# SwiGLU feed-forward on one core: the first weight slices move from two DMA queues to SyncE's alone

## The chip, the core and the metric

The kernel runs on one core of a Trainium2 chip. The metric is the device time of one execution in microseconds (us), lower is better. A core has five engines that run side by side, each with its own instruction stream: TensorE (PE; its weight loads are listed apart as PEld), VectorE (DVE), ScalarE (ACT), GpSimd (POOL) and SyncE (SP). A load or store is a DMA: an engine issues it in its own queue (here SyncE's, SPq, and ScalarE's, ACTq), 16 DMA engines move the data, and a semaphore tells when it has landed.

## What is computed

```python
# x: 1 x 2048 x 640, w_gate and w_up: 640 x 1536, w_down: 1536 x 640, all bfloat16
def reference(x, w_gate, w_up, w_down):
    g = _silu(x @ w_gate)
    u = x @ w_up
    return (g * u) @ w_down
```

## The kernel before

**Tiling.** The 2048 rows of x are worked in four blocks of 512 (`sb`), the 1536 hidden columns in twelve chunks of 128 (`fc`), the depth 640 in five chunks of 128 (`kd`). For each block and chunk, `proj` (L193 to L201) runs five matmuls of gate weights and five of up weights against the transposed x (`xT`, depth on the partitions), each filling a PSUM tile (`pg`, `pu`) of 128 x 512. `gate` (L208 to L215) applies silu on ScalarE (L212) and multiplies on VectorE (L213); the result `aT` feeds the down projection (L270 and L299). VectorE also works out the last four rows of x by itself (`row_dots`, L148), beside all this.

**How x is transposed.** Rows 0 to 255 are loaded as they are (`load_x`, L86, one DMA of 128 rows each), and transposed by TensorE in `transpose_chunk` (L186), from where ScalarE and VectorE copy them into `xT` (L191). All other rows come transposed by a DMA through the crossbar (`turn_x`, L110, a DMA_TRANSPOSE): rows 256 to 511 at the start, and each later block by one such load. In the text "the crossbar load" is that of rows 256 to 511.

**The start.** `head` (L217 to L251) writes out the order of TensorE's work on the first block and the first two chunks, and `keep_order` holds it: 18 warm-up matmuls on a tile of ones (L177), ten transposes of x rows 0 to 255 (L186), two more warm-up matmuls, 14 "early" gate matmuls (L237: 8 of 128 columns with the first two depth chunks, 6 of 256 columns with the other three), ten up matmuls over columns 0 to 255 (L195), and then, for each of the two chunks, five gate and five up matmuls over columns 256 to 511 (L195). These last need the crossbar load; the "late gate matmuls" are the first five of them. From then on the loop over blocks and chunks follows, with 512 columns per matmul.

**The order of the loads.** SyncE and ScalarE issue their DMAs in program order. The weights come in slices of hidden columns, `W_CHUNKS` = chunks 0 to 1, 2 to 3, 4 to 7 and 8 to 11, a gate and an up slice each. The first slices (256 columns, 320 KB each) are cut at depth chunk `K_CUT` = 2 into a part of 128 KB and one of 192 KB, and spread over both queues (L116 to L120):

- SyncE: x rows 0 to 127 (L86), gate depth 0 to 1 (L120), up depth 2 to 4 (L120), the crossbar load (L110), and then all later slices (L83), w_down (L126), the next block's crossbar load and the rest.
- ScalarE: x rows 128 to 255 (L86), gate depth 2 to 4 (L120), up depth 0 to 1 (L120), and then its first activation (L122), ahead of which it loads its table.

`turn_x(PE_X, SUB)` is the call that issues the crossbar load. The kernel has eight semaphores for these DMAs, taken in turn: a DMA that takes one again waits for the DMA that had it before, eight DMAs earlier.

Of the kernel before, what the change touches and what calls it, by code (L numbers as in the profile page):

```python
# [10 lines left out]
def _body(  # L11
# [8 lines left out]
    nc = tc.nc  # L20
# [12 lines left out]
    KD = D // P  # L33
# [10 lines left out]
    K_CUT = 2  # L44
    ROW_J = 0
    W_CHUNKS = [(0, 2), (2, 4), (4, 8), (8, 12)]
# [12 lines left out]
    wg_sb = consts.tile([P, KD, F], bf16)  # L59
    wu_sb = consts.tile([P, KD, F], bf16)  # L60
# [14 lines left out]
    wg_v = w_gate.rearrange("(kd p) f -> p kd f", p=P)  # L75
    wu_v = w_up.rearrange("(kd p) f -> p kd f", p=P)
    wd_v = w_down.rearrange("(kf p) d -> p kf d", p=P)

    def wslice(a, b):
        return slice(a * P, b * P)  # L80

    def load_w(eng, dst, src, a, b):
        eng.dma_start(out=dst[:, :, wslice(a, b)], in_=src[:, :, wslice(a, b)])  # L83
# [24 lines left out]
    def turn_x(c0, c1):  # L108
        s_sl = slice(c0 * P, c1 * P)
        nc.sync.dma_start_transpose(out=xT[:, :, s_sl], in_=xt_v[s_sl])  # L110
# [1 line left out]
    load_x(nc.sync, 0, 1)  # L112
    load_x(nc.scalar, 1, 2)
    f_sl = wslice(*W_CHUNKS[0])
    for dst, src, first, second in (
        (wg_sb, wg_v, nc.sync, nc.scalar),  # L116
        (wu_sb, wu_v, nc.scalar, nc.sync),
    ):
        for eng, k_sl in ((first, slice(0, K_CUT)), (second, slice(K_CUT, KD))):
            eng.dma_start(out=dst[:, k_sl, f_sl], in_=src[:, k_sl, f_sl])  # L120
    turn_x(PE_X, SUB)
    nc.scalar.activation(silu_first[:], ones[:, 0:1], ACT.Silu)  # L122
    for a, b in W_CHUNKS[1:]:
# [6 lines left out]
    def turn_w(dst, src):  # L130
# [7 lines left out]
        out=x_row[:],  # L138
        in_=x2[S - T : S, :].rearrange("t d -> (t d)").partition_broadcast(P),
# [114 lines left out]
    for sb in range(NSB):  # L254
# [27 lines left out]
        for q in range(P // Q):  # L282
            nc.scalar.dma_start(
                out=out2[
                    sb * S_BLK : sb * S_BLK + n_t, DA + q * Q : DA + (q + 1) * Q
                ].rearrange("(i r) c -> r i c", r=Q),
                in_=ot_q[q * Q : (q + 1) * Q, :].rearrange("r (i c) -> r i c", c=Q),
            )

        for j in range(SUB):  # L290
# [5 lines left out]
            for c0, c1, tag in cols:  # L296
# [10 lines left out]
                if c1 < D:  # L307
                    nc.scalar.copy(ot[:], po[:])  # L308
                    eng = nc.sync
                else:  # L310
                    nc.vector.tensor_copy(out=ot[:], in_=po[:])  # L311
                    eng = nc.scalar
# [81 lines left out]
def kernel(tc, *args):  # L394
    _body(tc, *args)
    tc.close()
    tc.compile()
    _trim(tc.nc)
# [30 lines left out]
```

## Time and profile before

| what | value |
|---|---|
| three runs, median (lowest to highest) | 163.66 us (163.46 to 163.86) |
| profiled execution: span from first to last instruction | 162.2 us |
| what lies around it (median less span) | 1.5 us |
| TensorE busy | 159.8 us, 798 matmuls |
| VectorE busy | 110.9 us |
| ScalarE busy | 42.7 us |
| gate and up matmuls of L195 | 58.5 and 59.8 us |
| DMA traffic | 15.86 MB, mean 98 GB/s |
| first matmul that reads w_up | starts at 5.80 us |
| first matmul that reads the crossbar load | starts at 6.92 us |

The profile is that of one execution; its own time isn't listed apart from its span, so the 1.5 us is the difference to the runs' median. "Busy" is the time in which an engine had an instruction under way. The chain that ended last is followed back from the last instruction: at each step to what released it, or to the instruction before it on its engine; the view gives shares of the span. The table of waits adds up, for each pair, how long an engine sat idle and what ended that. The timeline lists instructions in order of time: start, duration, engine, line, operation, output <- input, shape and count, all in us from the span's start. The DMA view lists issues with their sizes and the median time from issue to landing.

### The profile page before, as it was taken

The page shows a single profiled execution, that of the slowest core. Times are in us where ns is not written, and L with a number is a line of the kernel's source. Part 1 is how long each engine was busy: PE and PEld are TensorE (multiplying, and loading weights), DVE is VectorE, ACT ScalarE, POOL GpSimd, SP SyncE. Part 2 cuts the span into 40 slices and gives each one's busy share as a digit, 9 for nine tenths or more (in the row PEclk, how much of TensorE's full clock was granted, in tenths as well). Part 3 has the DMA queues.
Part 4 walks back from the last instruction along what each step waited for, and adds up shares of the span by engine and source line. Part 5 has one row for each costly group of instructions (what it writes and reads, how often), then busy time and mean ns, then how long its engine had stood idle before and what let it go on. Part 6 is the DMA issues. An engine that isn't in the chain of part 4 may idle for free.

```text
span 162.2 us, 2118 instructions
## 1 busy us (share of the span) xinstructions
PE 159.8 (99%) x798; PEld 77.9 (48%) x798; DVE 110.9 (68%) x249; ACT 42.7 (26%) x74; POOL 0.6 (0%) x6
## 2 busy tenths in 40 slices
PE   9999999999999999999999999999999999999995
PEld 8854444444444444444444444444444444445454
DVE  2042233599469999979919999979964999993000
ACT  5132222112222222221222322221214222222121
POOL 1000000000000000000000000000000000000000
PEclk9999999999999999999999999999999999999999
DMA  7999999994179992003110000000320000000312
GB/s 208 258 339 348 362 218 249 219 234 94 34 185 178 224 195 61 4 0 34 65 65 0 0 4 2 0 0 2 63 69 32 0 0 0 0 0 4 50 39 73
DMA packets 42441, 15.86 MB, mean 98 GB/s; under 512 B 33216, under 2 KB 42304, under 8 KB 42432
## 3 DMA queue, kind: packets, MB, share of 16 engines
q1 hardware_dynamic: 33536, 14.72, 37.7%
q10 hardware_dynamic: 8896, 1.02, 4.1%
q8 instruction: 6, 0.10, 0.2%
q14 instruction: 3, 0.02, 0.1%
HBM read 6.88 MB, written 2.62 MB: 59 GB/s over the span
## 4 chain that ended last, share of the span: by engine, by line
PE 99%; DVE 0%; issue 0%
PE pu L195 32%; PE pg L195 31%; PE po_a L299 26%; PE po_t L270 6%; PE pw L177 1%; PE pg L237 1%; PE pt L186 1%; DVE ot_b L311 0%; DVE ones L106 0%
## 5 line engine op out<-in xcount | busy, mean ns | idle before, releaser
L195 PE MATMUL pu<-xT,wu_sb 128*128 128x512 bf16 (+2 forms) x250 | 59.8, 370 | 0.0
L195 PE MATMUL pg<-xT,wg_sb 128*128 128x512 bf16 (+2 forms) x240 | 58.5, 374 | 0.0
L213 DVE TENSOR_TENSOR aT<-sg,pu 128x512 bf16<-128x512 f32 (+1 forms) x48 | 32.8, 683 | 32.8 <-PE pu L195 28.1
L212 ACT ACTIVATE sg<-pg 128x512 f32<-128x512 f32 (+1 forms) x48 | 28.6, 596 | 71.2 <-PE pg L195 68.1
L299 PE MATMUL po_a<-wd_sb,aT 128*128 128x512 bf16 (+2 forms) x216 | 42.8, 358 | 0.0
L148 DVE SCALAR_TENSOR_TENSOR prod<-wgT,x_row 128x640 f32<-128x640 bf16 x48 | 39.4, 821 | 1.1
L148 DVE SCALAR_TENSOR_TENSOR prod<-wuT,x_row 128x640 f32<-128x640 bf16 x48 | 39.4, 822 | 1.0
L195 PEld LDWEIGHTS <-wu_sb 128*128 128x128 bf16 x250 | 24.4, 98 | 27.6 <-DMA wu_sb<-in_w_up_dram 0.3
L195 PEld LDWEIGHTS <-wg_sb 128*128 128x128 bf16 x240 | 23.5, 98 | 26.9
L299 PEld LDWEIGHTS <-aT 128*128 128x128 bf16 x216 | 20.7, 98 | 21.6
L308 ACT CAST ot<-po_a 128x512 bf16<-128x512 f32 (+1 forms) x17 | 9.5, 560 | 32.0 <-PE po_a L299 20.8
L270 PE MATMUL po_t<-aT,wd_sb 128*128 128x512 bf16 (+1 forms) x48 | 10.4, 366 | 0.0
L270 PEld LDWEIGHTS <-wd_sb 128*128 128x128 bf16 x48 | 4.7, 98 | 5.1
L311 DVE CAST ot_b<-po_a 128x128 bf16<-128x128 f32 x1 | 0.3, 291 | 9.9 <-PE po_a L299 9.9
L279 ACT CAST ot_t<-po_t 128x512 bf16<-128x512 f32 (+1 forms) x4 | 2.2, 558 | 11.6 <-PE po_t L270 11.6
L148 DVE DVE_READ_ACCUMULATOR prod<-wuT,x_row 128x1 f32 x48 | 3.9, 82 | 0.0
L148 DVE DVE_READ_ACCUMULATOR prod<-wgT,x_row 128x1 f32 x48 | 3.9, 82 | 0.0
L281 DVE STREAM_TRANSPOSE ot_q<-ot_t 128x512 bf16<-128x512 bf16 (+1 forms) x4 | 2.7, 678 | 1.7 <-ACT ot_t L279 1.7
L177 PE MATMUL pw<-ones 128*128 128x128 bf16 x20 | 2.5, 313 | 0.4 <-DVE ones L106 0.4
L191 DVE COPY xT<-pt 128x384 bf16<-128x384 bf16 x2 | 0.7, 358 | 2.9 <-PE pt L186 2.9
L237 PE MATMUL pg<-xT,wg_sb 128*128 128x128 bf16 (+1 forms) x14 | 2.3, 360 | 0.0
L177 PEld LDWEIGHTS <-ones 128*128 128x128 bf16 x20 | 2.1, 148 | 0.4 <-DVE ones L106 0.4
(15 smaller groups left out, 7.6 us busy)
## 6 DMA issues: line engine op xcount, KB each, us to landing
wd_sb<-in_w_down_dram SPq DMA_DIRECT2D x1, 1920.0 KB, 14.5
out_dram<-ot SPq DMA_DIRECT2D x15, 128.0 KB, 1.7
wg_sb<-in_w_gate_dram SPq DMA_DIRECT2D x2, 640.0 KB, 7.7
wu_sb<-in_w_up_dram SPq DMA_DIRECT2D x2, 640.0 KB, 8.7
x_row<-in_x_dram SPq DMA_DIRECT2D x1, 640.0 KB, 4.7
out_dram<-ot_q ACTq DMA_DIRECT2D x12, 32.0 KB, 1.9
wg_sb<-in_w_gate_dram SPq DMA_DIRECT2D x1, 320.0 KB, 4.9
wu_sb<-in_w_up_dram SPq DMA_DIRECT2D x1, 320.0 KB, 5.4
```

The costliest lines, as they stand in the source:

```text
L148: nc.vector.scalar_tensor_tensor(out=prod[:], in0=wT[:, fc, :], scalar=1.0, in1=x_row[:, t, :], op0=ALU.mult, op1=ALU.mult, accum_out=acc[ ...
L177: nc.tensor.matmul(pw[:, 0:P], lhsT=ones[:], rhs=ones[:], start=True, stop=True)
L186: nc.tensor.transpose(out=pt[:, kd - k0, :], in_=x_sb[:, c, kd * P : (kd + 1) * P], identity=ident[:],)
L195: nc.tensor.matmul(ps[:, c0:c1], lhsT=w_sb[:, kd, fc * P : (fc + 1) * P], rhs=xT[:, kd, sb * S_BLK + c0 : sb * S_BLK + c1], start=(kd == 0 ...
L212: nc.scalar.activation(sg[:, 0:n_s], pg[:, 0:n_s], ACT.Silu)
L213: nc.vector.tensor_tensor(out=aT[:, fc, s0 : s0 + n_s], in0=sg[:, 0:n_s], in1=pu[:, 0:n_s], op=ALU.mult)
L237: nc.tensor.matmul(pg[:, c0:c1], lhsT=wg_sb[:, kd, wslice(fc, fc + 1)], rhs=xT[:, kd, c0:c1], start=(kd == 0 and c0 == 0), stop=(kd == KD ...
L270: nc.tensor.matmul(po_t[:], lhsT=wd_sb[:, kf, DA:D], rhs=aT[:, kf, sb * S_BLK : sb * S_BLK + n_t], start=(kf == 0), stop=(kf == KF - 1),)
L279: nc.scalar.copy(ot_t[:], po_t[:])
L281: nc.vector.transpose(out=ot_q[:], in_=ot_t[:])
L299: nc.tensor.matmul(po[:], lhsT=aT[:, kf, s0 : s0 + P], rhs=wd_sb[:, kf, c0:c1], start=(kf == 0), stop=(kf == KF - 1),)
L308: nc.scalar.copy(ot[:], po[:])
```

## The change

The four DMAs of the first gate and up slices become three, all issued by SyncE: gate depth 0 to 1, gate depth 2 to 4, and the whole up slice in one DMA by `load_w` (a helper that exists before, L83). They stand where SyncE's two parts stood, so the crossbar load comes behind all of them in SyncE's queue. ScalarE issues x rows 128 to 255 alone and goes on to its first activation. No instruction of TensorE, VectorE or GpSimd is changed, and what is computed stays the same.

```diff
     load_x(nc.sync, 0, 1)
     load_x(nc.scalar, 1, 2)
     f_sl = wslice(*W_CHUNKS[0])
-    for dst, src, first, second in (
-        (wg_sb, wg_v, nc.sync, nc.scalar),
-        (wu_sb, wu_v, nc.scalar, nc.sync),
-    ):
-        for eng, k_sl in ((first, slice(0, K_CUT)), (second, slice(K_CUT, KD))):
-            eng.dma_start(out=dst[:, k_sl, f_sl], in_=src[:, k_sl, f_sl])
+    for k_sl in (slice(0, K_CUT), slice(K_CUT, KD)):
+        nc.sync.dma_start(out=wg_sb[:, k_sl, f_sl], in_=wg_v[:, k_sl, f_sl])
+    load_w(nc.sync, wu_sb, wu_v, *W_CHUNKS[0])
     turn_x(PE_X, SUB)
     nc.scalar.activation(silu_first[:], ones[:, 0:1], ACT.Silu)
```

## The prediction

> **What bounds the kernel now.** First the page: its busy time and its chain of waits.
>
> ```profile
> span 162.2 us, 2118 instructions
> ...
> PE 159.8 (99%) x798; PEld 77.9 (48%) x798; DVE 110.9 (68%) x249; ACT 42.7 (26%) x74; POOL 0.6 (0%) x6
> ...
> PE 99%; DVE 0%; issue 0%
> ```
>
> TensorE (PE) is busy in 99% of the span and carries 99% of the chain that ended last. A load matters only where a matmul waits for it. So I looked next at the table of who waited for whom, for anything on PE or its weight loads (PEld) that ends on a DMA. There is one row:
>
> ```profile
> PEld L195 <- DMA wu_sb<-in_w_up_dram: 0.3, 1, 0.3
> ```
>
> Once, for 0.3 us, a weight load waited for the first slice of w_up, one of the loads that this change moves. The timeline of the first 8 us says how much of that PE lost (start, duration, engine, line, operation). From it I took SyncE's issues (SPq), ScalarE's (ACTq) and three matmul groups:
>
> ```profile
> 0.00 0.40 SPq L86 DMA_DIRECT2D x_sb<-in_x_dram  x1
> 0.12 0.41 ACTq L86 DMA_DIRECT2D x_sb<-in_x_dram  x1
> ...
> 0.46 0.42 SPq L120 DMA_DIRECT2D wg_sb<-in_w_gate_dram  x1
> 0.57 0.45 ACTq L120 DMA_DIRECT2D wg_sb<-in_w_gate_dram  x1
> ...
> 0.92 0.47 SPq L120 DMA_DIRECT2D wu_sb<-in_w_up_dram  x1
> 1.04 0.51 ACTq L120 DMA_DIRECT2D wu_sb<-in_w_up_dram  x1
> 1.43 1.63 SPq L110 DMA_TRANSPOSE xT<-in_x_dram  x1
> ...
> 3.11 0.57 SPq L83 DMA_DIRECT2D wg_sb<-in_w_gate_dram  x1
> ...
> 3.61 2.34 PE L237 MATMUL pg<-xT,wg_sb 128*128 128x128 bf16 x14
> ...
> 5.80 1.29 PE L195 MATMUL pu<-xT,wu_sb 128*128 128x256 bf16 x10
> ...
> 6.92 0.71 PE L195 MATMUL pg<-xT,wg_sb 128*128 128x256 bf16 x5
> ```
>
> The reader is to see three meeting points. The DMA view gives issue to landing, which I add to the issue times:
>
> - w_gate, first part (128 KB): 0.46 + 2.8 = 3.3; second part (192 KB): 0.57 + 3.6 = 4.2. The 14 early gate matmuls begin at 3.61, and the first of them that needs the second part at 4.47. No wait.
> - w_up: 1.04 + 4.7 = 5.7 (ScalarE's part) and 0.92 + 4.7 = 5.6. The up matmuls begin at 5.80.
> - the crossbar load (turn_x of x rows 256 to 511): 1.43 + 5.4 = 6.8. The first matmul that reads it starts at 6.92. This is the closest one: 0.1 us to spare.
>
> **The change part by part, with costs.**
>
> *w_up, the wait that goes.* Without the wait PE would go on when its 14 gate matmuls are through. The 18 warm-up matmuls of 128 columns start at 0.40 and the next group at 2.29: 105 ns each. Eight of the 14 have 128 columns and six 256: 8 x 0.105 + 6 x 0.21 = 2.1 us, so they are done with the array at 3.61 + 2.1 = 5.72 to 5.75. The up matmuls start at 5.80. PE itself lost 0.05 us; the rest of the 0.3 is PEld, which runs ahead. So **at most 0.05 us** can be won here at PE's present pace.
>
> Does w_up land in time? Ahead of its end stand x (320 KB), w_gate (320 KB) and itself (320 KB), 0.98 MB. The rates of the half-microsecond stretches from 1.0 to 4.5 us (159, 352, 322, 254, 282, 284, 315 GB/s) sum to 0.98 MB, so the data is in at about 4.5 us, whichever queue holds it. One queue alone is no slower: from 6.5 to 8.3 us only SyncE's queue moves data, 275 GB/s. Data to landing is about 0.5 us (the crossbar load's last 256-byte packet ends at 6.29 in the DMA records, and it lands at 6.82). So w_up lands at 4.9 to 5.2, ahead of 5.72. It stays ahead up to 0.5 us of error; past that the 0.05 is not won.
>
> *w_gate.* Its second part goes to SyncE, issued at 0.92 instead of 0.57. It no longer shares with w_up, which now stands behind it. x, w_gate: 640 KB by the same rates is in at about 3.4, landed at 3.8 to 4.0, needed at 4.36 (its weight load). Nothing.
>
> *ScalarE.* It loses two issues (0.45 + 0.51 us) and starts its table load (1.28 us, now at 1.58) at about 0.6. What it does next, the copy of transposed x at 2.99, would be ready some 0.25 us sooner, but the gate matmul that reads it starts only when PE has passed the transposes and two gap matmuls. PE is busy there, so nothing.
>
> *The crossbar load, moved past one more issue.* SyncE now issues x, two gate parts (0.42 and 0.45 to 0.47) and the whole w_up slice (320 KB; the row at 3.11 for that shape takes 0.57). Issues start at 0.00, 0.46, 0.92, 1.43 and, for turn_x, **2.03 instead of 1.43**. In its ring it stands behind 320 KB of w_up instead of 192. No trace row shows this order, so I bound the landing:
>
> - earliest: data starts when w_up's is in, 4.5. From 5.5 to 6.0 us, with nothing but this load moving, 566 packets went: 1,132 per us. Its 1,280 packets (256 rows of 1,280 bytes by 256) take 1.13 us: 5.6, landed 6.1.
> - latest: the same 5.4 us from issue as now, 2.03 + 5.4 = 7.4. A little under it lies its own stretch of now, 4.10 (first packet in the DMA records) to 6.82, 2.7 us, from 4.5: 7.2. That stretch holds a stop: 760 packets in the microsecond from 4.1, then 62 in the 0.3 us from 5.1.
> - nearest row: the crossbar load of 512 rows issued at 44.88 has its first packet at 46.18 and lands at 5.1 from issue, 49.98, 3.8 us for 2,560 packets. Half of it is 1.9: 6.4.
>
> I take 6.6, between the nearest row and the row that holds the stop. PE, with the 0.05 won, needs it at 6.87. So it stays hidden, by a quarter of a microsecond; past 6.87 every 0.1 us of lateness costs 0.1.
>
> The Trainium skill (DMA: Bandwidth & Descriptors, Latency and other measured facts) gives 261 GB/s for a transposing DMA with a non-contiguous middle dimension, by which these 0.33 MB would take an estimated 1.26 us and land at about 6.3; the load's own stretch here, 2.7 us, is 120 GB/s and does not agree.
>
> *What is queued behind.* The next slices go out after turn_x, so some 0.6 us later: 3.71 instead of 3.11 for w_gate columns 256 to 511. But their data waits for the crossbar load's anyway. That slice lands at 3.11 + 4.9 = 8.0 now and its matmuls start at 9.11; w_up's at 3.73 + 5.4 = 9.1 against 10.19. Both have 1 us of cover, more than the 0.6. The slices behind (10.9 and 13.0 against 13.4 and 14.5) have more than that. All later issues keep their order, and nothing that PE does changes.
>
> **Sum.** -0.05 (w_up) + 0 + 0 + 0 = -0.05 us: the span goes from 162.17 to 162.12. The three runs have a median of 163.66, 1.5 above the profiled span, for start and end, which the change leaves alone: **163.6 us**.
>
> **The rivals.**
>
> *Slower: the crossbar load is late.* One mechanism: its landing follows its issue, not the bytes ahead, so 0.6 us later issue means 7.2 to 7.4. It decides from 6.87 on. PE would start the late gate matmuls 0.1 after landing, at 7.5 instead of 6.92: +0.4 to +0.6, 164.0 to 164.3. For it: the load is now the closest of all, and its issue is the only thing that moves back. Against it: now its first packet leaves only at 4.10, 2.7 us after the issue, against 1.3 at 44.88, so it waits in the ring, not for the issue.
>
> *Faster: PE's slow phase ends sooner in other executions.* The matmuls start 105 ns apart per 128 columns early on, but from 9.11 to 10.19 five of 512 columns take 1.08 us, 54 ns per 128. The pace doubles about when the up matmuls start (between 5.5 and 5.9), though the profile's granted clock reads 1.00 throughout. If in another execution it doubles 1 to 2 us sooner, PE reaches the up matmuls 0.5 to 1 us sooner; the kernel before can't use that, as w_up lands at 5.7. The changed kernel can, until the crossbar load's landing: the late gate matmuls start at 6.5 to 6.7 instead of 6.92, -0.25 to -0.45 us, 163.2 to 163.4. For it: the runs lie 0.4 us apart, and something moves them. Against it: it needs both an early doubling and a crossbar load by 6.5, and the one trace has the doubling at 5.5 to 5.9. The Trainium skill (TensorE: Matmul & The Clock Gate, Part 1: The HAM clock gate) has a rule for this rival: the clock doubles at the end of a busy 3.4 us window that runs free of the kernel's start, so its place would differ from run to run; one trace can't show that.
>
> *Nothing at all:* the parts of w_up are held by the crossbar load's traffic in the new order too and land at 5.6 or later: 0, 163.7. This has the forecast's sign within what can be told.
>
> **How the numbers follow.** About 0.2% (0.33 us) is what a measurement of this kernel can tell from no change. Forecast and "nothing at all" together 0.46; the crossbar load late by over 0.33 us net 0.27; the early doubling with a gain over 0.33 us 0.27. Unlike signs hold much of the chance, so the forecast's own range is 163.4 to 163.8. The whole range goes down to 163.1 (the faster rival at its full 0.45 and 0.1 for the runs' spread) and up to 164.25 (the slower rival at 0.6).
>
> **What would show it.** In the profile after: w_up landing by 5.2, with no PEld row waiting for it; turn_x issued near 2.03 and landed by 6.87; the late gate matmuls within 0.1 us of 6.87; the chain still 99% PE. A PE or PEld row that waits for xT's DMA, or late gate matmuls past 7.1, would show the slower rival; up matmuls at 5.5 or sooner and late gate matmuls by 6.6 the faster one. The forecast is wrong if matmuls from 9 us on wait for weights, which would mean the covers of 1 us did not hold.

## The result and the profile after

| kernel | median of 10 runs each | lowest to highest |
|---|---|---|
| before | 163.51 us | 163.14 to 163.86 |
| changed | 164.27 us | 163.95 to 164.51 |

The change makes the kernel slower by 0.76 us, ratio 1.005 (95% interval 1.0039 to 1.006). The forecast was -0.05 us at 163.6, 163.4 to 163.8 as its own range; the time lies just over the top of the whole range, 164.25. The profiled execution has a span of 163.0 against 162.2.

The page of the changed kernel, its span, the busy time and the chain that ended last, by engine and by line:

```profile
span 163.0 us, 2117 instructions
...
PE 159.7 (98%) x798; PEld 77.6 (48%) x798; DVE 110.9 (68%) x249; ACT 42.9 (26%) x74; POOL 0.6 (0%) x6
...
PE 95%; DMA 3%; SPq 1%; DVE 0%; issue 0%
PE pu L192 32%; PE pg L192 31%; PE po_a L296 26%; PE po_t L267 6%; DMA wu_sb<-in_w_up_dram 3%; SPq L116 1%; SPq L86 0%; DVE ot_b L308 0%
```

PE works as long as before (159.7 against 159.8 us). What is new is in the chain: 3% is a DMA, the first w_up slice, and 1% the issue of the gate parts ahead of it. So the time was added in the start, by waiting, and the table of waits says for what:

```profile
PEld L234 <- DMA wg_sb<-in_w_gate_dram: 0.8, 1, 0.8
PE pg L234 <- DMA wg_sb<-in_w_gate_dram: 0.6, 1, 0.6
...
PEld L183 <- DMA x_sb<-in_x_dram: 0.5, 1, 0.5
PEld L192 <- DMA wu_sb<-in_w_up_dram: 0.4, 1, 0.4
...
PE pt L183 <- DMA x_sb<-in_x_dram: 0.2, 1, 0.2
...
PE pu L192 <- DMA wu_sb<-in_w_up_dram: 0.2, 1, 0.2
```

PE now waits for both slices that were moved. It also waits 0.2 us for x rows, whose load was not moved; e1 comes back to that. The timeline of the changed kernel places it (line numbers are three lower than before):

```profile
0.45 0.93 SPq L116 DMA_DIRECT2D wg_sb<-in_w_gate_dram  x2
0.54 1.28 ACT L119 ACT_TABLE_LOAD   x1 [0.54 <-issue]
...
1.42 0.49 SPq L83 DMA_DIRECT2D wu_sb<-in_w_up_dram  x1
...
1.95 3.29 SPq L110 DMA_TRANSPOSE xT<-in_x_dram  x1
...
3.96 0.92 PE L234 MATMUL pg<-xT,wg_sb 128*128 128x128 bf16 x8
...
5.47 0.83 PE L234 MATMUL pg<-xT,wg_sb 128*128 128x256 bf16 x6 [0.59 <-DMA wg_sb<-in_w_gate_dram]
...
6.46 1.26 PE L192 MATMUL pu<-xT,wu_sb 128*128 128x256 bf16 x10 [0.16 <-DMA wu_sb<-in_w_up_dram]
...
7.74 0.71 PE L192 MATMUL pg<-xT,wg_sb 128*128 128x256 bf16 x5
```

The up matmuls start at 6.46 instead of 5.80 and the late gate matmuls at 7.74 instead of 6.92. That 0.82 is the whole difference of the spans; the next group starts at 9.91 against 9.11 and nothing is lost or regained behind it. The DMA view of the changed kernel (issue to landing) gives the landings:

```profile
wu_sb<-in_w_up_dram SPq DMA_DIRECT2D x1, 320.0 KB, 5.0
wg_sb<-in_w_gate_dram SPq DMA_DIRECT2D x1, 192.0 KB, 4.5
...
xT<-in_x_dram SPq DMA_TRANSPOSE x1, 5.7
```

w_gate's second part: 0.91 + 4.5 = 5.4 (before 4.2). w_up: 1.42 + 5.0 = 6.4 (5.7). The crossbar load: 1.95 + 5.7 = 7.7 (6.8). All three are late, and the w_up slice alone holds PE until 6.46 + ten matmuls at 0.11 = 7.57; the crossbar load, landed at 7.69, adds the last 0.17.

Why are they late, with the same bytes? The busy time by stretches of 0.75 us shows it (stretch, its length, PE busy and instructions, granted clock, DMA share, GB/s), first of the kernel before:

```profile
2.50:3.25 0.75, 0.75 (x9) 1.00 0.94 268
3.25:4.00 0.75, 0.75 (x10) 1.00 0.99 278
4.00:4.75 0.75, 0.75 (x9) 1.00 1.31 304
```

and of the changed kernel:

```profile
2.50:3.25 0.75, 0.54 (x6) 1.00 1.00 280
3.25:4.00 0.75, 0.75 (x10) 1.00 0.69 186
4.00:4.75 0.75, 0.75 (x10) 1.00 0.86 181
```

From 3.25 us the DMA engines move a third less, and are busy for 0.69 of the time where they were for 0.99, though every load of the first slices had been issued by 1.91. This hole is what the experiments are about.

### The profile page after: what moved, and what is told of

It is laid out like the page before. It is cut to its first block, busy times and chain, and to the rows that moved or that the text cites. A ratio compares the mean times of both kernels' runs of the same rounds, so it can differ in the third digit from the quotient of the medians.

```text
span 163.0 us, 2117 instructions
## 1 busy us (share of the span) xinstructions
PE 159.7 (98%) x798; PEld 77.6 (48%) x798; DVE 110.9 (68%) x249; ACT 42.9 (26%) x74; POOL 0.6 (0%) x6
## 3 DMA queue, kind: packets, MB, share of 16 engines
HBM read 6.88 MB, written 2.62 MB: 58 GB/s over the span
## 4 chain that ended last, share of the span: by engine, by line
PE 95%; DMA 3%; SPq 1%; DVE 0%; issue 0%
PE pu L192 32%; PE pg L192 31%; PE po_a L296 26%; PE po_t L267 6%; DMA wu_sb<-in_w_up_dram 3%; SPq L116 1%; SPq L86 0%; DVE ot_b L308 0%
## 5 line engine op out<-in xcount | busy, mean ns | idle before, releaser
L234 PE MATMUL pg<-xT,wg_sb 128*128 128x128 bf16 (+1 forms) x14 | 1.7, 280 | 0.6 <-DMA wg_sb<-in_w_gate_dram 0.6
```

The costliest lines, as they stand in the source:

```text
L234: nc.tensor.matmul(pg[:, c0:c1], lhsT=wg_sb[:, kd, wslice(fc, fc + 1)], rhs=xT[:, kd, c0:c1], start=(kd == 0 and c0 == 0), stop=(kd == KD ...
```

## The experiments

All numbers in one table. "Rate" is the GB/s from 3.25 to 4.00 us. "Copies" is the start of the last of the 1,280 packets of 512 bytes that carry the first gate and up slices, "crossbar" the landing of the crossbar load, both from the DMA records and semaphores of the one profiled execution (us). The ratio is to the kernel before on the same chip.

| kernel | rate | copies | crossbar | median us | ratio (95%) |
|---|---|---|---|---|---|
| before | 278 | 5.12 | 6.82 | 163.51 | |
| changed | 186 | 6.00 | 7.69 | 164.27 | 1.005 (1.0039 to 1.006) |
| e1, changed | 152 | 6.17 | 7.87 | 164.47, one run | |
| e9, changed | 198 | 5.97 | 7.67 | 164.17 | 1.003 (1.0013 to 1.0048) |
| e2 up on ScalarE | 343 | 4.60 | 6.31 | 163.92 | 1.0044 (1.0014 to 1.0074) |
| e3 late issue | 330 | 4.58 | 6.57 | 163.69 | 1.002 (1.0002 to 1.0038) |
| e4 plain x | 106 | | | 165.22 | 1.0107 (1.0068 to 1.0146) |
| e5 gate part on ScalarE | 290 | 5.57 | 7.31 | 163.51 | 0.9968 (0.9927 to 1.0008) |
| e6 up part on ScalarE | 290 | 5.19 | 6.86 | 163.75 | 1.0019 (0.9975 to 1.0063) |
| e7 gate part and up on ScalarE | 216 | 8.14 | 9.11 | 168.26 | 1.0219 (1.011 to 1.0328) |
| e8 gate in one | 305 | 4.93 | 6.65 | 163.97 | 1.0026 (0.9999 to 1.0053) |
| e10 gate in one | 317 | 5.35 | 7.07 | 163.69 | 1.0016 (0.9995 to 1.0036) |
| e11 cut at 1 | 240 | 5.74 | 7.44 | 165.92 | 1.0126 (1.0077 to 1.0175) |
| e12 cut at 4 | 272 | 4.95 | 6.64 | 163.70 | 1.0011 (0.9994 to 1.0028) |
| e13 x on ScalarE | 353 | 4.89 | 6.57 | 165.05 | 1.0083 (1.005 to 1.0116) |
| e14 cut at 4, part on ScalarE | 296 | 4.73 | 6.41 | 163.62 | 0.9993 (0.9977 to 1.001) |
| e15 tiny between | 143 | 5.92 | 7.59 | 164.63 | 1.0084 (1.005 to 1.0119) |

**e1: is it of the change?** The changed kernel, nothing edited.

> The changed kernel as it is, for a second profile. What has to come back if it is of the change and not of one execution: the second part of w_gate lands after 4.8 us (5.42 in the first profile of it), w_up after 6.0 (6.42), the crossbar load after 7.3 (7.69). What may differ: x rows 0 to 127 landed at 2.66 there against 2.25 in the kernel before, though nothing ahead of them changed; if that is of one execution, they land by 2.4 here. About 164.3 us either way.

The second gate part landed at 5.46, w_up at 6.60, the crossbar load at 7.87: it is of the change. x rows 0 to 127 landed at 2.66 again, against 2.25 in the profile before; but e3, whose first loads are those of the kernel before, has 2.55, and e12 2.13. So I don't count it to the change, and PE waits for gate behind it in any case.

**e2: the up slice in the other queue.**

```diff
-    load_w(nc.sync, wu_sb, wu_v, *W_CHUNKS[0])
+    load_w(nc.scalar, wu_sb, wu_v, *W_CHUNKS[0])
```

> The changed kernel with the whole first w_up slice in ScalarE's queue behind x rows 128 to 255; both gate parts stay on SyncE's, and the crossbar load is issued at about 1.43 again. Theory A (the copies ahead end late when they all stand in one queue, and the crossbar load can't flow before the last of them has ended): copies spread over two queues end by 5.2, the crossbar load lands by 7.0, 163.4 to 163.7. Theory B (the crossbar load lands a fixed time after its issue): 1.43 + 5.4 = 6.8, the same 163.4 to 163.7. If a whole w_up slice in one DMA is itself the trouble: over 164.0.

The copies and the crossbar load came as early as theory A says; 6.31 is half a microsecond sooner than theory B has it. The time did not follow: 163.92. The view of waits has PE waiting 0.35 us for the second gate part, which landed at 5.21: ScalarE issued w_up at 0.53, SyncE the gate part at 0.91, and w_up's packets went first. Whether that comes from the order of issue, or from the gate part's place as the third load of SyncE's queue (e15 below), this run doesn't tell. Theory B gets its own run next.

**e3: the issue alone is late.** The kernel before with this ahead of `turn_x(PE_X, SUB)`:

```diff
+    tiny = consts.tile([P, 2, 8], bf16)
+    for n in range(2):
+        nc.sync.dma_start(out=tiny[:, n, :], in_=x_v[:, 0, n * 8 : n * 8 + 8])
     turn_x(PE_X, SUB)
```

> The kernel before, with two tiny loads (16 bytes per partition, into a tile that nothing reads) on SyncE's queue just ahead of the crossbar load, so that it is issued 0.8 to 1.0 us later, 2.2 to 2.4 instead of 1.43, and all else stays on both queues. Theory A (it waits for the last copy ahead, not for its issue): landing within 0.2 us of 6.8, 163.4 to 163.8. Theory B (fixed time after its issue): lands at 7.6 to 7.8, late gate matmuls at 7.7 to 7.9, 164.3 to 164.5.

The crossbar load became the ninth DMA of eight semaphores, and so was issued later than meant. From the timeline and the DMA view of e3, its issue and its time to landing:

```profile
3.01 1.46 SPq L110 DMA_TRANSPOSE xT<-in_x_dram  x1
```

```profile
xT<-in_x_dram SPq DMA_TRANSPOSE x1, 3.6
```

Issued 1.6 us later than before, it landed at 6.57, 0.25 us *sooner*. Theory B, a fixed time from issue, is refuted. The 0.2% that e3 loses has its own row in the timeline of e3: the next gate slice, issued behind the crossbar load, is late now.

```profile
9.33 1.25 PE L198 MATMUL pg<-xT,wg_sb 128*128 128x512 bf16 x4 [0.37 <-DMA wg_sb<-in_w_gate_dram]
```

**e4: no transposing load behind the copies.** The crossbar load of the changed kernel is a plain load here, which leaves these rows untransposed:

```diff
-    turn_x(PE_X, SUB)
+    nc.sync.dma_start(
+        out=xT[:, :, PE_X * P : SUB * P],
+        in_=x2[PE_X * P : SUB * P, :]
+        .rearrange("(p two) d -> p (two d)", two=2)
+        .rearrange("p (k c) -> p k c", k=KD),
+    )
```

> The changed kernel with the crossbar load replaced by a plain load of the same 320 KB into the same tile, so that these rows are not transposed and the outputs of rows 256 to 511 are not the reference's; it tells what the copies do without a transposing load behind them. If one queue alone makes the copies end late: w_gate's second part still lands after 4.8 and w_up after 6.0, about 163.8 to 164.2. If it is the crossbar load behind them that holds them up: w_gate's second part by 4.2, w_up by 5.3, 163.0 to 163.5.

The hole is there without the crossbar load, deeper even. The stretches of e4:

```profile
2.50:3.25 0.75, 0.75 (x8) 1.00 0.78 201
3.25:4.00 0.75, 0.75 (x10) 1.00 0.51 106
```

w_gate's second part landed at 5.26 and w_up at 7.17, so the kernel is slower than expected, 165.22. The 16 increments of w_up's semaphore came between 4.62 and 7.17: the DMA engines have drifted apart by 2.5 us, and those that were ahead went on with the next slices. The crossbar load does not make the hole.

**e5 and e6: half undone.** In e5 the second gate part, in e6 the first up part is back in ScalarE's queue:

```diff
-    nc.sync.dma_start(out=wg_sb[:, K_CUT:KD, f_sl], in_=wg_v[:, K_CUT:KD, f_sl])
+    nc.scalar.dma_start(out=wg_sb[:, K_CUT:KD, f_sl], in_=wg_v[:, K_CUT:KD, f_sl])
```

```diff
-    load_w(nc.sync, wu_sb, wu_v, *W_CHUNKS[0])
+    nc.scalar.dma_start(out=wu_sb[:, 0:K_CUT, f_sl], in_=wu_v[:, 0:K_CUT, f_sl])
+    nc.sync.dma_start(out=wu_sb[:, K_CUT:KD, f_sl], in_=wu_v[:, K_CUT:KD, f_sl])
```

> The change half undone: gate depth 2 to 4 back in ScalarE's queue behind x rows 128 to 255; gate depth 0 to 1 and the whole up slice on SyncE's. Theory A' (a single queue leaves the DMA engines without work from about 2.7 to 4 us, while its next load is not yet being served, and only loads of the other queue fill that): the 192 KB of ScalarE's queue fill it, 250 GB/s or more from 3.25 to 4.00 us instead of 150 to 190, w_gate's second part lands by 4.4, the crossbar load by 7.0, 163.4 to 163.7. Theory D (the loss grows with the bytes that stand in SyncE's queue ahead of the crossbar load: 480 KB before, 800 KB in the change, 608 here): 0.4 of the loss stays, 163.8 or 163.9.

> The other half undone: up depth 0 to 1 (128 KB) back in ScalarE's queue behind x rows 128 to 255; both gate parts and up depth 2 to 4 on SyncE's. Theory A': 128 KB fill most of the hole, 230 GB/s or more from 3.25 to 4.00 us, the crossbar load by 7.1; but the gate part is served later, about 4.4 to 4.9, so PE may wait for it for 0.1 to 0.3 us: 163.5 to 163.9. Theory D (672 KB ahead): 0.6 of the loss stays, 163.9 to 164.0.

Either half fills the hole (290 GB/s in both) and brings the loss back to nothing that can be told: 163.51 and 163.75, intervals that hold 1. Runs on this chip scattered, from 163 to 165.6 in the kernel before too, so between 163.5 and 163.9 they don't decide. e5's profiled execution, at 163.9 a longer one, has the gate part at 5.47 and the crossbar load at 7.31, later than expected. So a rate without a hole is not all that a landing needs: 15 of the 16 increments of that gate part's semaphore had come by 4.14, and a single late DMA engine held back the last to 5.47.

**e7: both parts on ScalarE, the crossbar load with little ahead of it.**

```diff
-    for k_sl in (slice(0, K_CUT), slice(K_CUT, KD)):
-        nc.sync.dma_start(out=wg_sb[:, k_sl, f_sl], in_=wg_v[:, k_sl, f_sl])
-    load_w(nc.sync, wu_sb, wu_v, *W_CHUNKS[0])
+    nc.sync.dma_start(out=wg_sb[:, 0:K_CUT, f_sl], in_=wg_v[:, 0:K_CUT, f_sl])
+    nc.scalar.dma_start(out=wg_sb[:, K_CUT:KD, f_sl], in_=wg_v[:, K_CUT:KD, f_sl])
+    load_w(nc.scalar, wu_sb, wu_v, *W_CHUNKS[0])
```

> A version that may beat both: SyncE's queue has x rows 0 to 127, gate depth 0 to 1 and the crossbar load (288 KB ahead of it); ScalarE's has x rows 128 to 255, gate depth 2 to 4 and the whole up slice. Theory A': both queues have work from 2.7 to 4 us, over 270 GB/s there; w_gate's second part by 4.4, w_up by 5.4, the crossbar load by 6.7: 163.2 to 163.6. Theory D: less ahead than in the kernel before, 163.0 to 163.4. If the transposing load, now free to start sooner, holds up w_up's copies on the other queue: w_up after 5.8 and over 163.7.

Hoped for as the best, it is the worst: 168.26. The crossbar load got to the DMA engines first, and w_up, on the other queue, landed at 8.86; PE waited 2.8 us for it. From the stretches of e7:

```profile
4.00:4.75 0.75, 0.43 (x6) 1.00 0.17 22
```

For most of a microsecond next to nothing moved, and the crossbar load itself landed at 9.11. A transposing load among copies of another queue cost more here than the change itself (ratio 1.0219 against 1.005).

**e8 and e10: the gate slice in one load.** Same queue, same bytes, one DMA less:

```diff
-    for k_sl in (slice(0, K_CUT), slice(K_CUT, KD)):
-        nc.sync.dma_start(out=wg_sb[:, k_sl, f_sl], in_=wg_v[:, k_sl, f_sl])
+    load_w(nc.sync, wg_sb, wg_v, *W_CHUNKS[0])
     load_w(nc.sync, wu_sb, wu_v, *W_CHUNKS[0])
```

> The changed kernel with the first gate slice in one DMA of 320 KB instead of two parts, all on SyncE's queue still; the same bytes in the same order in one DMA less. If the hole lies at the third DMA of the queue, whatever it is: w_gate's own data covers more of the time until w_up is served; over 220 GB/s from 3.25 to 4.00 us, and the crossbar load lands by 7.4; the early gate matmuls wait for the whole slice instead of a part (0.1 to 0.4 us of it stays): 163.8 to 164.2. Theory D (800 KB ahead): as the change, 164.2 to 164.4.

> The first gate slice in one DMA again, all on SyncE's queue. Theory C (the hole opens when the queue's second load is read out before its third is served, at about 3.3 us; a second load of 320 KB lasts until then, one of 128 KB doesn't): no hole again, over 270 GB/s from 3.25 to 4.00 us, the crossbar load by 6.9, 163.4 to 163.8 against 164.2 to 164.5 for two parts. Theory D (bytes of the queue ahead, 800 KB in both): the same time as two parts, 164.2 to 164.5.

> The changed kernel as it is, for its time and profile on the same chip as the next three. 164.2 to 164.5; from 3.25 to 4.00 us the DMA engines move under 200 GB/s; the crossbar load lands 1.7 us after the start of the last of the 1,280 packets of 512 bytes that carry the first w_gate and w_up slices, at 7.5 to 7.9.

The hole is gone, with everything still on SyncE's queue. The stretch of e10, and behind it that of e9, the changed kernel on the same chip:

```profile
3.25:4.00 0.75, 0.75 (x9) 1.00 1.15 317
```

```profile
3.25:4.00 0.75, 0.75 (x10) 1.00 0.72 198
```

The crossbar load lands at 7.07, in e8 at 6.65, against 7.67. In time the step is less sharp: 163.69 against 164.17, ratios whose intervals overlap (0.9995 to 1.0036 and 1.0013 to 1.0048). By rate and landing, then, neither the single queue nor the 800 KB ahead of the crossbar load is the cause by itself: that is against theory D, and e12 below, with the same 800 KB and 163.70, is too. What counts is how the first 320 KB are cut.

**e11 and e12: the cut moved, as many loads.** `slice(0, 1), slice(1, KD)` and `slice(0, 4), slice(4, KD)` in place of `K_CUT`: 64 + 256 KB and 256 + 64 KB instead of 128 + 192.

> The changed kernel with the gate slice cut at depth chunk 1 instead of 2, 64 KB and 256 KB, so that the second load of SyncE's queue is the smallest; the same bytes and as many DMAs. Theory C: the second load is read out at about 2.4 instead of 2.7 us, the hole is 0.2 to 0.4 us longer, under 150 GB/s from 2.50 to 3.25 us, the crossbar load at 7.8 to 8.2: 164.4 to 164.9. Theory E (only the number of DMAs counts, not their sizes): as the change, 164.2 to 164.5.

> The changed kernel with the gate slice cut at depth chunk 4, 256 KB and 64 KB: the second load of SyncE's queue lasts longer, the third is small; as many DMAs. Theory C: the second load lasts until about 3.1, so there is hardly a hole before the third; if a fourth load (w_up) is served later still than the third, the 64 KB of the third leave a hole behind it instead. Over 240 GB/s from 2.50 to 3.25 us, the crossbar load by 7.1, 163.6 to 164.0, if there is no second hole. Theory E: as the change, 164.2 to 164.5.

A large part first: no hole (294 and 272 GB/s from 2.50 to 4.00), 163.70. A small part first: slower, 165.92. Theory E falls, as sizes count at the same number of loads. Theory C had the order right, but its picture of e11 is not confirmed: the profiled execution, 164.04 and the shortest of four (up to 166.38), shows 242 and 240 GB/s, not the deep hole expected. What the longer runs of e11 lost, no trace shows.

**e13 and e15: place in the queue.** In e13 x rows 0 to 127 go to ScalarE's queue (`load_x(nc.scalar, 0, 1)`), so the second gate part is second in SyncE's instead of third. In e15 2 KB between the parts make it fourth:

```diff
     nc.sync.dma_start(out=wg_sb[:, 0:K_CUT, f_sl], in_=wg_v[:, 0:K_CUT, f_sl])
+    nc.sync.dma_start(out=tiny[:], in_=x_v[:, 0, 0:8])
     nc.sync.dma_start(out=wg_sb[:, K_CUT:KD, f_sl], in_=wg_v[:, K_CUT:KD, f_sl])
```

> The changed kernel with x rows 0 to 127 in ScalarE's queue too, ahead of rows 128 to 255: SyncE's queue has gate depth 0 to 1, gate depth 2 to 4, the up slice and the crossbar load, so that the second gate part is its second load. x rows 0 to 127 share the DMA engines with gate from the start and land 0.2 to 0.4 us later. Theory C (the third load of a queue is served late): the second gate part follows the first without a hole, over 250 GB/s from 2.50 to 3.25 us, and the hole, if any, comes at w_up, about 3.2; the crossbar load by 7.1, 163.5 to 163.9. Theory F (a queue alone leaves holes, whatever the place of the load): under 220 GB/s from 2.50 to 4.00 us, the crossbar load at 7.4 or later, 164.1 to 164.6.

> The changed kernel with a load of 16 bytes per partition (2 KB in all, into a tile that nothing reads) on SyncE's queue between the two gate parts, so that the second gate part is the fourth load and not the third, and is issued 0.5 us later. Theory C: the tiny load takes the third place and covers nothing; the hole is as long or longer, under 200 GB/s from 2.50 to 4.00 us; w_gate's second part lands 0.2 us or more later and the crossbar load at 7.7 to 8.2, 164.3 to 165.0. Theory F: 2 KB change nothing, as the change, 164.1 to 164.5.

The 2 KB do what theory C says: the hole starts at 2.50 and is the deepest of those with a crossbar load. The stretches of e15:

```profile
2.50:3.25 0.75, 0.75 (x9) 1.00 0.56 123
3.25:4.00 0.75, 0.75 (x10) 1.00 0.54 143
4.00:4.75 0.75, 0.74 (x8) 1.00 1.12 311
```

164.63. The landings did not go as expected: 5.01 for the gate part, sooner than the 5.42 of the first profile of the changed kernel, and 7.59 for the crossbar load. In e13 there is no hole (362 and 353 GB/s) and the crossbar load lands at 6.57; but x rows 0 to 127, sharing with gate, land at 3.42, more than the 0.2 to 0.4 us later that was expected, PE starts its transposes at 3.47, and that costs more than all else: 165.05, missed. ScalarE's queue was at work until 3.75 in e13, so theory F is refuted by e10 and e12, not by this run.

**e14: both means at once.** Gate depth 0 to 3 on SyncE, depth 4 on ScalarE, up on SyncE.

```diff
+    nc.sync.dma_start(out=wg_sb[:, 0:4, f_sl], in_=wg_v[:, 0:4, f_sl])
+    nc.scalar.dma_start(out=wg_sb[:, 4:KD, f_sl], in_=wg_v[:, 4:KD, f_sl])
+    load_w(nc.sync, wu_sb, wu_v, *W_CHUNKS[0])
```

> The gate slice cut at depth chunk 4: 256 KB on SyncE's queue as its second load, 64 KB on ScalarE's behind x rows 128 to 255; the whole up slice on SyncE's. Theory C: the second load lasts until the third is served, ScalarE's part lands early, no hole (over 270 GB/s from 2.50 to 4.00 us), w_up by 5.5, the crossbar load by 6.8: 163.2 to 163.6, level with the kernel before or 0.1% under it. If it is slower than 163.8, two queues are no help once the sizes are right.

No hole, and the crossbar load at 6.41, 0.4 us sooner than in the kernel before. The time is that of the kernel before, ratio 0.9993 (0.9977 to 1.001). By then PE waits for x (landed at 2.62) and for the larger gate part (4.22), so the earlier landing buys nothing that can be told.

## Why the prediction was wrong, point by point

1. *w_up, and the step that failed.* "[...] so the data is in at about 4.5 us, whichever queue holds it. One queue alone is no slower: from 6.5 to 8.3 us only SyncE's queue moves data, 275 GB/s." The row was right for its stretch, in which large loads had been issued long before, and wrong for the start. From 3.25 to 4.75 us the single queue moved 186 and 181 GB/s, and the copies ended at 6.0, not 4.5. w_up landed at 6.4 where the forecast had 4.9 to 5.2. The prediction added up bytes; what was short was not bandwidth but work at hand for the DMA engines, which were busy for 0.69 of the time from 3.25 to 4.00 us. They did not all lack it alike: of the 16 increments of the second gate part's semaphore, eight had come by 3.70 us and the last came at 5.42, and a load has landed only with its last. At 4.75 us 277 of the 1,280 packets of the copies were still to start (16 in the kernel before), and these 0.14 MB took until 6.00. That they were left to the DMA engines that were behind fits this, but the records don't name the DMA engine of a packet. In the kernel before, the two queues cover each other: in its DMA records SyncE's queue starts 11 and 16 packets of 512 bytes in the two quarters of a microsecond from 2.75, while ScalarE's starts 116 and 129.
2. *w_gate.* Same step, "landed at 3.8 to 4.0, needed at 4.36 (its weight load). Nothing." It landed at 5.42, and PE waited 0.59.
3. *ScalarE.* Right: the table load starts at 0.54, and it wins nothing.
4. *The crossbar load.* The issue was right (1.95, forecast 2.03), the landing was not: 7.69, past even the bound of 7.4. Taken was 6.6, which rested on copies that end at 4.5. In 14 of the 16 profiles that have this load it lands 1.67 to 1.74 us after the start of the last copy, from 4.60 + 1.71 (e2) to 6.17 + 1.70 (e1); e3 (1.99, issued at 3.01) and e7 (0.97, copies of the other queue) are the others. That is the step of the bound called earliest (1.13 us of packets and 0.5 to land); the middle value that was taken had the load itself too slow and the copies too early. Its packets that start earlier stand: in the changed kernel single ones take up to 1.55 us, where the median is 18 ns.
5. *What is queued behind.* Right in what came of it, by less than it says: the next slices were issued from 5.29 on, not 3.71, as the issue of the crossbar load took 3.29 us. They landed at 9.12 and 10.22 and were needed at 9.91 and 10.99, so the cover fell from 1 to 0.8 us and held, with PE itself 0.8 us late. e3 shows where it ends: issued 1.4 us later than before, the gate slice is late by 0.37 us.
6. *The rivals.* The slower one had the sign and, in part, the place; its mechanism, landing follows issue, is refuted by e3, and its price of 0.4 to 0.6 was short of the 0.8. That its 164.0 to 164.3 holds the measured 164.27 is luck. The faster one got its early doubling (see the last section), but it needed earlier loads too and got none. "Nothing at all" had w_up at 5.6 or later; it came at 6.4, which no longer costs nothing.
7. *The sum.* Its base was high: what lies around the span is about 1.3 us, not 1.5, in every run that lists both (164.29 and 163.0 for the changed kernel's profiled one), and ten runs of the kernel before have a median of 163.51. The change itself was forecast at -0.05 and measured at +0.76.

The Trainium skill (DMA: Bandwidth & Descriptors, Issuing engines are not separate DMA queues) says that DMAs of all engines run on the same 16 DMA engines and that issuing from several only saves issue time. That would have made this change cost next to nothing. The measurement decides otherwise for the first microseconds: 278 against 186 GB/s for the same bytes, all issued by 1.91 us. With larger early loads one queue moved as much as two (317 GB/s in e10).

What is shown: the hole is there with all slices in one queue (three profiles of the changed kernel, e4, e15), it does not come from the crossbar load (e4), it goes if the second queue has a part (e2, e5, e6), and it goes in the single queue if its early loads are larger (e8, e10, e12). What stays open is why: that a queue needs some time per load before the next one flows on all 16 DMA engines, so that small early loads are read out faster than the next ones come, fits all but e11's profile and the one late DMA engine of e5. What sets the DMA engines apart stays open too; no trace shows the inside of a queue.

## What to carry to other kernels

In the first microseconds, count loads and not only bytes: a queue whose early loads are small can leave the DMA engines without work even if everything has been issued (186 GB/s against 278 here), and a second queue (290), or larger early loads (317), filled that. A bandwidth that was read from the steady stretch of the trace did not hold for the start here; look at the rate of each queue in short stretches there, and at the last increment of a load's semaphore as well as the middle one. And the transposing load here landed about 1.7 us after the last plain copy ahead of it had started, hardly moved by its issue, so the copies' end is what to shorten.

## What the runs showed of the hardware that was not expected

- A crossbar load on one queue and copies on the other nearly stopped each other in e7's profile: 22 GB/s for 0.75 us.
- The pace of PE doubles at a place that differs from run to run. In two profiles of the changed kernel the eight gate matmuls of 128 columns take 0.92 us from 3.96 (the first) and 0.71 us from 3.81 (e9), with starts 107 ns apart that become 56 at 4.6 and at 4.0 us. In e7 eight from 3.70 us are at the fast pace (0.73 us with the last one's tail); in e13, where PE had stood idle for 0.98 us, fourteen from 5.12 us are still at the slow one (2.34 us, as long as those of the kernel before). The Trainium skill (TensorE: Matmul & The Clock Gate, Part 1: The HAM clock gate) says that the window that decides this runs free of the kernel's start; the two profiles of one kernel agree with that.
- The 261 GB/s that the Trainium skill (DMA: Bandwidth & Descriptors, Latency and other measured facts) gives for a transposing DMA, which the prediction set aside, is near what the load reaches once the copies are out of the way: with only the crossbar load's packets moving, 281 GB/s from 6.25 to 6.75 us in the changed kernel.
